# A linear-attention and SwiGLU block, two layers: the MLP's last product too by seven block products, in two passes of row tiles

## The chip, the cores and the metric

The kernel runs on one core of one Trainium2 chip. The metric is the device time of one execution in microseconds. Each kernel is run several times, and the median counts. One more execution of each kernel was profiled; durations and stalls quoted here come from that execution.

## The reference

```python
def _A_ref(x, wqkv, wo):            # S = 2048, D = 512, 32 heads of 16
    q, k, v = heads(x @ wqkv)
    phi = lambda t: where(t > 0, t + 1, exp(t)) + 1e-6
    pq, pk = phi(q), phi(k)
    kv = einsum("bhsd,bhse->bhde", pk, v)
    z = einsum("bhsd->bhd", pk)
    num = einsum("bhqd,bhde->bhqe", pq, kv)
    den = einsum("bhqd,bhd->bhq", pq, z)[..., None] + 1e-6
    return merge_heads(num / den) @ wo

def _B_ref(x, w1, w3, w2):          # F = 1792
    return (silu(x @ w1) * (x @ w3)) @ w2

x = A_x
x = x + _A_ref(_layernorm(x), A_wqkv, A_wo)
x = x + _B_ref(_layernorm(x), B_w1, B_w3, B_w2)
x = x + _A_ref(_layernorm(x), A_wqkv, A_wo)
x = x + _B_ref(_layernorm(x), B_w1, B_w3, B_w2)
```

All inputs are float32, and both layers use the same weights.

## The kernel before

Every float32 matrix is held as two float16 parts, a high and a low one, and each product runs as three float16 products (high by high, low by high, high by low; `PASSES`, `mm`). The high part is a copy on ScalarE, the low part a subtraction on VectorE (`split`).

The work goes in this order, twice: keys and the state (`attn_keys`, `state_in`, `state_out`), queries and weighing (`query`, `weigh`), attention output (`attn_out`), then the MLP. `pair` is one layer. In layer 0 a generator, `prepare`, converts weights in between, and during the MLP a second one, `background`, converts the rest; `PACE` says how many steps of them are put between two pieces of other work. The order that each engine gets comes from a scheduler in the framework, with priorities (`later` lowers one); TensorE then works in that order.

In the MLP, x has 16 tiles of 128 rows, in four chunks of four tiles (`NC`), and F has 14 tiles of 128, in seven groups of two (`NG`). One block of work is one group for one chunk; there are 28 in a layer. For w1 and w3 the kernel already uses the seven products of Winograd's form of Strassen's algorithm in place of eight: rows (`mlp_rows`) and weights (`w13_group`) are prepared as seven combinations each, and a block runs seven products P1 to P7 on three PSUM banks (`ba`, `bb`, `bc`), 12 matmuls of 256 columns each. ScalarE copies the bank `bb` out four times in a block (L740, L747, L750, L757), VectorE adds the other two (L744, L751, L755), and `swiglu` makes two halves of the hidden values, early and late: a tanh, two products, a copy and a subtraction (L709 to L714), 512 columns each.

The last product, by w2, is plain: `mlp_out` adds the block's hidden values times two tiles of w2 to four PSUM banks `po`, one for each row tile of the chunk, with 24 matmuls of 512 columns. TensorE does this one block later, between the seven products of the next one. After a set's last group `finish` adds each bank to x on VectorE (L832) and, in the end, stores the row tile (L836). Layer 0 runs the groups in two sets, 0 to 2 and 3 to 6, each for all chunks, so that weights can be converted during the first set; layer 1 runs all seven groups for one chunk after another. All 14 tiles of w2 stay in SBUF during an MLP.

DMAs go out through SyncE's queue in its own order: row transposes (L692, L697), raw weights (L334, L434), and rows kept in DRAM for a second set (L701, L779).

Of the kernel before, what the change touches and what calls it, by code (L numbers as in the profile page):

```python
# [45 lines left out]
GROUP = 14 * KB  # L46
AT_W = 0
AT_W2 = AT_W + NG * GROUP
AT_X = AT_W2 + 28 * KB
# [4 lines left out]
AT_H = AT_T + 4 * KB  # L54
AT_END = AT_H + 6 * KB
# [20 lines left out]
def kernel(  # L76
# [40 lines left out]
    def bank(name):  # L117
        return psum.tile([P, 512], F32, tag="w", name=name)

    nat_ring = Ring(view, *span(AT_NAT, 3), *span(AT_W2 + 16 * KB, 3))  # L120
# [5 lines left out]
            nat_ring,  # L126
# [4 lines left out]
            Ring(view, *span(AT_W2 + 16 * KB, 3)),  # L131
# [10 lines left out]
    t_ring = Ring(view, *span(AT_T, 2))  # L142
    h_ring = Ring(view, *span(AT_H, 3))
    xk_ring = Ring(view, *span(XB0 + 8 * KB, 3))
    xq_ring = Ring(view, *span(AT_W2 + 22 * KB, 3))
    pt_first = (*span(XB0 + 8 * KB, 3), XB1 + 12 * KB)
    pt_ring = Ring(view, *span(AT_W2 + 8 * KB, 4))
# [9 lines left out]
    ident = const.tile([P, P], F32, name="ident")  # L157
# [5 lines left out]
    mask = const.tile([P, P], F32, name="mask")  # L163
# [21 lines left out]
    wq_s = view(AT_W2, F16, 2, NK, D)  # L185
    wo_s = view(AT_W2 + 8 * KB, F16, 2, NK, D)
# [4 lines left out]
    w13 = [view(AT_W + g * GROUP, F16, 2, 2, 2, 7, P) for g in range(NG)]  # L191
    w2_s = [view(AT_W2 + f * 2 * KB, F16, 2, D) for f in range(NF)]
    st_att = [view(AT_W + at * KB, F32, NK, D) for at in (18, 0, 26, 34)]
    st_w13 = view(AT_W + 42 * KB, F32, 2, 2, 2, F)
    raw_at = {3: AT_W + 70 * KB, 4: AT_W + 78 * KB, 5: AT_W + 86 * KB, 6: rows_at[0]}
# [3 lines left out]
    w2_d = dram.tile([P, NF, 2, D], F16, name="w2_d")  # L199
# [127 lines left out]
    def load_raw(g):  # L327

        dst = view(raw_at[g], F32, 2, 2, 2, 2, P)
# [6 lines left out]
    def w13_group(g):  # L336

        dst = w13[g]
        if g in raw_at:
            raw = view(raw_at[g], F32, 2, 2, 4, P)  # L340
# [35 lines left out]
    def prepare():  # L376
# [37 lines left out]
        info["w2"] = weight_scale("w2", parts["w2"], 2.0**14)  # L414
        cb = scaled(info["w1"][1], 2.0**-9)
# [4 lines left out]
        for g in SETS[0]:  # L420
            yield from w13_group(g)
            state["groups"] = g + 1

    state = {"groups": 0, "tiles": 0, "rows": 0}
    w2_stage = (
        Ring(view, *span(AT_W2 + 24 * KB, 2)),
        Ring(view, *span(AT_W + 94 * KB, 2)),
    )

    def w2_pair(g):  # L430

        for f in (g, NG + g):
            r = w2_stage[g > SETS[0][-1]].next(F32, D)
            nc.sync.dma_start(r, w2_rows[:, f, :])  # L434
            split(w2_s[f][:, 0, :], w2_s[f][:, 1, :], r, info["w2"][2])
            yield 1
        state["tiles"] = g + 1

    def background():

        for g in SETS[0]:
            yield from w2_pair(g)
        for g in (3, 4, 5):
            load_raw(g)
        for g in SETS[1]:
            yield from w2_pair(g)
        nc.sync.dma_start(w2_d, view(AT_W2, F16, NF, 2, D))
        for g in SETS[1]:
            if g == 6:
                while state["rows"] < NC:  # L450
                    yield 100
                load_raw(6)
            yield from w13_group(g)
            state["groups"] = g + 1
# [9 lines left out]
    PACE = (3, 1, 2, 4)  # L464
# [17 lines left out]
    def attn_keys(layer, ready, prep, before_gram):  # L482
# [3 lines left out]
        pks = {}  # L486
        xts, nats = ready
# [19 lines left out]
        for t in range(NT):  # L507
# [4 lines left out]
            pk = h_ring.next(F16, 2, D)  # L512
# [7 lines left out]
            if t == 0:  # L520
                before_gram()
                gt += [acc_bank(f"gt{j}") for j in range(NK)]
                if layer == 0:
                    pz.append(bank("pz"))
# [467 lines left out]
```

## Time and profile before

| | |
|---|---|
| median of 3 runs | 1286.61 us (1285.42 to 1288.26) |
| profiled execution | 1289.51 us, of which the span of its instructions is 1287.8 us |
| TensorE (PE) busy | 1193.8 us, 93% |
| VectorE (DVE) busy | 722.6 us, 56% |
| ScalarE (ACT) busy | 605.8 us, 47% |
| GpSimd (POOL) busy | 269.0 us, 21% |
| mean granted TensorE clock | 0.97 |

Times of instructions count from the span's start. PE is the matmul part of TensorE, PEld its weight loads, SP the queue of SyncE. Matmuls are pipelined: one alone lasts longer than the distance to the next, so their cost is read from the distance. A line of a group gives the source line, engine, operation, what it writes and reads with the shapes, the count, the total and mean duration, and the idle time of the engine just before with what ended it. The line of a helper stands for all its callers: nearly all matmuls are L310.

### The profile page before, as it was taken

The numbers are of one execution on the slowest core, as the hardware profiler recorded it, in microseconds if no ns is written. First come the engines' busy times: TensorE is split into PE (matmuls) and PEld (weight loads), VectorE is DVE, ScalarE is ACT, GpSimd is POOL, SyncE is SP. The second block draws the span as 40 slices with busy tenths as digits, with TensorE's granted clock in tenths as the row PEclk, the third lists the DMA queues.
The fourth block names the chain that finished last, engine by engine and source line by source line (L and its number), as shares of the span: only waits on it lengthen the run. The fifth ranks groups of instructions, "written<-read, shape, count | busy, mean of one in ns | idle before, by whom it ended". The sixth has DMA issues, their size and how long they took to land.

```text
span 1287.8 us, 18971 instructions
## 1 busy us (share of the span) xinstructions
PE 1193.8 (93%) x7752; PEld 763.6 (59%) x7752; DVE 722.6 (56%) x1164; ACT 605.8 (47%) x1048; POOL 269.0 (21%) x264
## 2 busy tenths in 40 slices
PE   2999697678999999999999998989998999999998
PEld 1444343356767777777764443446776777777775
DVE  4968959884465345453544239784435345434444
ACT  5667667664343333433346645665334333333332
POOL 3310357163110000100004523675004001000000
PEclk9999899789999999999999998999998999999999
DMA  7976566375051101010216323565003003000000
GB/s 208 349 215 222 138 156 164 86 235 130 34 143 58 58 1 58 1 58 9 66 42 164 98 50 91 108 159 102 1 1 91 2 1 85 6 1 19 16 1 33
DMA packets 160520, 111.33 MB, mean 86 GB/s; under 512 B 129329, under 2 KB 137521, under 8 KB 158257
## 3 DMA queue, kind: packets, MB, share of 16 engines
q1 hardware_dynamic: 160432, 110.13, 31.9%
q8 instruction: 60, 0.98, 0.3%
q14 instruction: 28, 0.22, 0.1%
HBM read 50.86 MB, written 27.79 MB: 61 GB/s over the span
## 4 chain that ended last, share of the span: by engine, by line
PE 70%; DVE 8%; DMA 8%; POOL 7%; ACT 4%; issue 3%; SPq 0%; DVEq 0%; POOLq 0%; ACTq 0%
PE po L310 21%; PE bb L310 20%; PE bc L310 10%; PE pk L310 6%; PE gt L310 6%; DMA arena<-arena 5%; PE ba L310 5%; POOL arena L696 3%; DMA arena<-in_B_w_dram 1%; DVE arena L479 1%; DVE arena L583 1%; PE pq L310 1%; DVE arena L589 1%; DVE arena L244 1%; POOL arena L594 1%
## 5 line engine op out<-in xcount | busy, mean ns | idle before, releaser
L310 PEld LDWEIGHTS <-arena 128*128 128x128 f16 x7704 | 757.7, 99 | 502.4 <-issue 60.4
L310 PE MATMUL po<-arena 128*128 128x512 f16 x1728 | 428.7, 386 | 25.0 <-DMA arena<-arena 17.9
L310 PE MATMUL bb<-arena 128*128 128x256 f16 x2688 | 343.7, 276 | 11.5 <-ACT arena L750 6.3
L310 PE MATMUL bc<-arena 128*128 128x256 f16 x1344 | 165.5, 276 | 9.6 <-ACT arena L757 9.4
L751 DVE TENSOR_TENSOR arena<-arena,bc 128x512 f32<-128x512 f32 x56 | 38.4, 685 | 206.0 <-ACT arena L750 206.0
L714 DVE TENSOR_TENSOR arena<-arena 128x512 f16<-128x512 f32 x112 | 83.9, 749 | 87.7 <-ACT arena L713 87.3
L713 ACT ACTIVATE arena<-arena 128x512 f16<-128x512 f32 x112 | 70.2, 627 | 128.9 <-DVE arena L711 128.9
L750 ACT ACTIVATE arena<-bb 128x512 f32<-128x512 f32 x56 | 33.3, 594 | 200.3 <-PE bb L310 200.3
L710 DVE SCALAR_TENSOR_TENSOR arena<-arena 128x512 f32<-128x512 f32 x112 | 78.3, 699 | 79.8 <-ACT arena L709 79.5
L696 POOL TENSOR_TENSOR arena<-arena 128x512 f16<-128x512 f32 (+2 forms) x48 | 70.7, 1493 | 234.5 <-DMA arena<-arena 232.2
L244 DVE SCALAR_TENSOR_TENSOR arena<-arena,scalars 128x512 f16<-128x512 f32 (+2 forms) x110 | 89.5, 838 | 36.1 <-ACT arena L243 35.9
L709 ACT ACTIVATE arena<-arena,scalars 128x512 f32<-128x512 f32 x112 | 80.7, 721 | 58.4 <-DVE arena L751 42.0
L310 PE MATMUL pk<-arena 128*128 128x512 f16 x384 | 92.6, 394 | 15.2 <-ACT arena L243 8.8
L243 ACT ACTIVATE arena<-arena,scalars 128x512 f16<-128x512 f32 (+2 forms) x110 | 74.3, 717 | 42.9 <-DMA arena<-in_B_w_dram 18.3
L310 PE MATMUL gt<-arena 128*128 128x512 f16 x384 | 90.6, 384 | 2.1 <-ACT arena L243 2.1
L310 PE MATMUL pq<-arena 128*128 128x512 f16 x384 | 88.2, 379 | 0.0
L310 PE MATMUL ba<-arena 128*128 128x256 f16 x672 | 87.7, 273 | 0.0
L711 DVE SCALAR_TENSOR_TENSOR arena<-arena 128x512 f32<-128x512 f32 x112 | 79.4, 709 | 3.4
L757 ACT ACTIVATE arena<-bb 128x512 f32<-128x512 f32 x56 | 33.3, 595 | 66.0 <-PE bb L310 65.9
L287 ACT ACTIVATE arena<-arena,nb_all,rs_all 128x512 f32<-128x512 f32 x64 | 50.7, 805 | 25.3 <-POOL arena L696 13.8
L280 POOL TENSOR_SCALAR ve<-mv_all 128x4 f32<-128x4 f32 (+2 forms) x9 | 4.1, 451 | 278.8 <-DVE mv_all L273 267.4
L301 POOL TENSOR_TENSOR arena<-arena 128x512 f16<-128x512 f32 x31 | 37.9, 1227 | 93.1 <-ACT arena L300 91.7
(112 smaller groups left out, 903.9 us busy)
## 6 DMA issues: line engine op xcount, KB each, us to landing
xt_d<-arena SPq DMA_DIRECT2D x32, 256.0 KB, 3.0
arena<-xt_d SPq DMA_DIRECT2D x32, 256.0 KB, 2.8
arena<-in_B_w_dram SPq DMA_DIRECT2D x8, 896.0 KB, 7.1
arena<-in_B_w_dram SPq DMA_DIRECT2D x28, 256.0 KB, 3.2
xb_d<-arena SPq DMA_DIRECT2D x4, 1792.0 KB, 6.4
arena<-xb_d SPq DMA_DIRECT2D x4, 1792.0 KB, 6.8
arena<-in_A_x_dram SPq DMA_DIRECT2D x16, 256.0 KB, 5.7
arena<-in_B_w_dram SPq DMA_DIRECT2D x32, 128.0 KB, 3.1
```

Source lines behind the costliest of these rows:

```text
L243: nc.scalar.activation(hi, src, AF.Copy, scale=scale)
L244: nc.vector.scalar_tensor_tensor(lo, src, scale, hi, OP.mult, OP.subtract)
L287: nc.scalar.activation(dst, x_sb[:, t, :], AF.Identity, scale=rs_all[:, t : t + 1], bias=nb_all[:, t : t + 1],)
L301: engine.tensor_tensor(nat[:, 1, :], xn, nat[:, 0, :], OP.subtract)
L310: nc.tensor.matmul(dst, lhs(a, k), rhs(b, k), start=first and k == 0 and i == 0, stop=last and k == n - 1 and i == len(PASSES) - 1, skip_g ...
L696: nc.gpsimd.tensor_tensor(nat[:, 1, lo:hi, :], s, nat[:, 0, lo:hi, :], OP.subtract)
L709: nc.scalar.activation(t, gate, AF.Tanh, scale=info["half_u1"])
L710: nc.vector.scalar_tensor_tensor(t, t, 1.0, gate, OP.add, OP.mult)
L711: nc.vector.scalar_tensor_tensor(t, up, 2.0**-48, t, OP.mult, OP.mult)
L713: nc.scalar.activation(hs[:, 0], t, AF.Copy)
L714: nc.vector.tensor_tensor(hs[:, 1], t, hs[:, 0], OP.subtract)
L751: nc.vector.tensor_tensor(early[:, 1, :], early[:, 1, :], bc, OP.add)
```

## The change

The product by w2 is made by the same seven block products. The hidden values of a block (two row halves by two F tiles) give seven combinations, w2's two tiles by two column halves give seven, and each of the seven products, 256 columns wide, is summed over a set's groups in half a PSUM bank. For one row tile of each half that fills three and a half banks, and four are given to this work, so a chunk is run in two passes: one for the first row tile of each half, with every group as its hidden values become ready, two blocks late, and one for the second row tiles after the set's last group, for all groups of the set in a row. Only at the end of a pass are the seven sums combined and added to x (`mlp_add`). So hidden values are kept for a whole set, in slots of 7 KB.

For that space the weights can no longer all stay in SBUF: there are four slots for groups of w1 and w3 and five for groups of w2. Layer 0 runs sets of 3, 2 and 2 groups, layer 1 of 3 and 4; groups that are converted and needed again are stored in DRAM and fetched. Layer 1 now keeps its rows in DRAM too.

```diff
+OUT = (((0, 0), (3, 5)), ((4, 2), (5, 1)), ((1, 3), (2, 6)), ((6, 4),))
-SETS = ((0, 1, 2), (3, 4, 5, 6))
+SETS = (((0, 1, 2), (3, 4), (5, 6)), ((4, 5, 6), (3, 0, 1, 2)))
+SLOT13 = {0: 0, 1: 1, 2: 2, 3: 3, 4: 0, 5: 1, 6: 2}
+SLOT2 = {0: 3, 1: 4, 2: 2, 3: 0, 4: 1, 5: 3, 6: 4}
...
-    PACE = (3, 1, 2, 4)
+    PACE = (3, 1, 2, 3)
...
+    def w2_group(g):
+
+        raw = w2_stage.next(F32, 4, HALF)
+        for i, f in enumerate((g, NG + g)):
+            nc.sync.dma_start(raw[:, 2 * i : 2 * i + 2, :], w2_rows[:, f, :])
+        dst, scale = w2_s[g], info["w2"][2]
+        yield 1
+        split(dst[:, 0, 0], dst[:, 1, 0], raw[:, 0], scale)
+        yield 1
+        split(dst[:, 0, 1:3], dst[:, 1, 1:3], raw[:, 2:4], scale)
+        yield 1
+        a11, a21, a12, a22 = (raw[:, i] for i in range(4))
+        for to, a, b, op in (
+            (a22, a21, a22, OP.add),
+            (a21, a11, a21, OP.subtract),
+            (a11, a22, a11, OP.subtract),
+            (a12, a12, a11, OP.subtract),
+        ):
+            W2ENG.tensor_tensor(to, a, b, op)
+        yield 1
+        split(dst[:, 0, 3:], dst[:, 1, 3:], raw, scale)
...
+    def background(first):
+
+        yield from first
+        a, b, c = SETS[0]
+        for g in a:
+            yield from w2_group(g)
+            store("w2", g, view(AT_W2 + SLOT2[g] * GROUP2, F16, GROUP2 // 2))
+        late = view(AT_W + 3 * GROUP, F16, 2, 2, 2, 7, P)
+        for g in b[::-1]:
+            load_raw(g)
+            if g == b[-1]:
+                for i in a:
+                    store("w13", i, view(AT_W + i * GROUP, F16, GROUP // 2))
             yield 1
+            yield from w13_group(g, late)
+            if g == b[-1]:
+                store("w13", g, view(AT_W + 3 * GROUP, F16, GROUP // 2))
+            have.add(("w13", g))
+            yield from w2_group(g)
+        while state["set"] < 1:
+            yield 100
+        for g in c:
+            load_raw(g)
+            yield 1
+            yield from w13_group(g, w13[g])
...
+    W2ENG = nc.gpsimd
+    TENG = (nc.vector, nc.vector)
...
+    def hidden_parts(hs, t, lo, hi):
+        nc.scalar.activation(hs[:, 0, lo:hi], t[:, lo:hi], AF.Copy)
+        nc.vector.tensor_tensor(hs[:, 1, lo:hi], t[:, lo:hi], hs[:, 0, lo:hi], OP.subtract)
+
+    def hidden(engine, hs, t, late):
+        swiglu(late, t[:, 2:4])
+        hidden_parts(hs, t, 0, 2)
+        b11, b22, b12, b21, t1, t2, t4 = (t[:, i] for i in range(7))
+        engine.tensor_tensor(t1, b12, b11, OP.subtract)
+        engine.tensor_tensor(t2, b22, t1, OP.subtract)
+        engine.tensor_tensor(b12, b22, b12, OP.subtract)
+        engine.tensor_tensor(t4, b21, t2, OP.subtract)
+        hidden_parts(hs, t, 2, 7)
...
-    def mlp_out(g, h, is_late, po, tiles, ends):
-        for i in tiles:
-            half, sub = divmod(i, 2)
...
+    def mlp_out(sub, g, hs, acc, ends):
+
+        cs = slice(sub * P, (sub + 1) * P)
+        w2 = w2_s[g]
+        for a, bs in ((0, (0, 1)), (1, (0,))):
+            for po, pair in zip(acc, OUT):
+                for i, (qw, qx) in enumerate(pair):
+                    for b in bs:
+                        nc.tensor.matmul(
+                            po[:, i * HALF : (i + 1) * HALF],
+                            hs[:, a, qx, cs],
+                            w2[:, b, qw, :],
...
+    def mlp_add(sub, c, acc, engine):
...
+        def add(dst, src, to):
+            nc.vector.scalar_tensor_tensor(dst, src, cb, to, OP.mult, OP.add)
+
+        nc.scalar.activation(u[:, 0], a0[:, :HALF], AF.Copy, scale=cb)
+        add(x0, a2.rearrange("p (h n) -> p h n", h=2), x0)
+        add(x1, a3[:, None, :HALF].to_broadcast([P, 2, HALF]), x1)
+        add(x1[:, 0], a1[:, HALF:], x1[:, 0])
+        add(u[:, 1], a0[:, HALF:], u[:, 0])
+        add(u[:, 2], a1[:, :HALF], u[:, 1])
+        engine.tensor_tensor(x0, x0, u[:, 0::2], OP.add)
+        engine.tensor_tensor(x1, x1, u[:, 1:], OP.add)
...
+                def middle(at_, i=i, first=at == 0 and i == 0):
+                    if first:
+                        first_pending(at_)
+                    if at_ == 0 and len(waiting) > 1:
+                        first_half(waiting.pop(0))
+                    if at_ == 2 and done:
+                        ends.append(second_half())
+                    if at_ == 3 and ends:
+                        ends.pop()()
...
+    def moves(layer, gs, i):
+
+        if layer == 0 and gs is SETS[0][0] and i == 0:
+            fetch("w13", 4, 0)
+        if layer == 1 and gs is SETS[1][0]:
+            fetch("w13", i, i)
+            if i == 0:
+                fetch("w2", 0, 2)
```

In the built program of the changed kernel, lines have new numbers: L322 is `mm`, L833 the products by w2, L764 to L770 `swiglu` and its splits, L776 to L779 the four differences, L851 and L853 the adds at the end of a half, L859 and L860 the two sums on the engine that is passed in (GpSimd, and VectorE for the last half).

More of the change, by code (lines that the diff above doesn't have):

```diff
@@ L811, in pair, with first_pending @@
                     steps(prep, PACE[1] if t < 9 else PACE[2])
-        more = background() if layer == 0 else iter(())
+        more = background(prep) if layer == 0 else iter(())
         def ready_for(what, g):
-            for source in (prep, more):
-                while state[what] <= g and next(source, None) is not None:
-                    pass
-        def pending(i):
+            while layer == 0 and (what, g) not in have:
+                next(more)
+        def first_pending(i):
             if i < 2:
```

296 lines of the change are left out of this document (161 added, 135 removed).

## The prediction

> **What bounds the kernel now.** I read the engine summary, then the two MLP stretches as time windows, then the order of instructions inside one block, then the groups by shape.
>
> ```profile
> PE 1193.8 (93%) x7752; PEld 763.6 (59%) x7752; DVE 722.6 (56%) x1164; ACT 605.8 (47%) x1048; POOL 269.0 (21%) x264
> ...
> 200.00:264.00 64.00, 47.73 (x236) 25.30 (x237) 57.37 (x102) 45.27 (x87) 23.34 (x21) 0.84 0.48 123
> 264.00:290.00 26.00, 17.99 (x110) 11.83 (x109) 22.73 (x24) 17.80 (x28) 20.56 (x17) 0.87 0.80 252
> 290.00:500.00 210.00, 203.62 (x1502) 148.27 (x1500) 103.75 (x154) 79.55 (x131) 19.35 (x18) 0.98 0.23 65
> 500.00:678.00 178.00, 175.69 (x1301) 127.09 (x1299) 87.04 (x145) 65.80 (x108) 14.32 (x17) 1.00 0.14 42
> ...
> 884.00:1277.00 393.00, 387.96 (x2888) 283.26 (x2886) 176.00 (x256) 144.74 (x237) 35.70 (x31) 0.99 0.09 21
> ```
>
> Columns of the windows: length, busy time of PE, PEld, DVE, ACT, POOL, clock, DMA. The first block of MLP one ends at 264, the second at 290; its last at 678; MLP two runs from 884 to 1277. In 884:1277 PE misses 5 us of 393: product time is the bound there. In 200:264 it is not: DVE is busy 57 of 64 us, PE 48, at a clock of 0.84.
>
> ```profile
> 1007.66 0.68 DVE L744 TENSOR_TENSOR arena<-arena,ba 128x512 f32<-128x512 f32 x1
> ...
> 1008.59 1.47 PE L310 MATMUL bb<-arena 128*128 128x256 f16 x12
> ...
> 1009.90 1.89 PE L310 MATMUL po<-arena 128*128 128x512 f16 x8
> ...
> 1011.63 0.60 PE L310 MATMUL bb<-arena 128*128 128x256 f16 x4
> ```
>
> Twelve products of 256 columns take 1009.90 − 1008.59 = 1.31 us, 109 ns each; eight of 512 take 1.73, 216 each. So a block now is 84 × 0.109 + 24 × 0.216 = 9.17 + 5.19 = 14.36 us.
>
> ```profile
> L714 DVE TENSOR_TENSOR arena<-arena 128x512 f16<-128x512 f32 x112 | 83.9, 749 | 87.7 <-ACT arena L713 87.3
> ...
> L751 DVE TENSOR_TENSOR arena<-arena,bc 128x512 f32<-128x512 f32 x56 | 38.4, 685 | 206.0 <-ACT arena L750 206.0
> ```
>
> **PE, the gain.** 42 products of 256 columns replace 24 of 512: 42 × 0.109 = 4.58 us, so a block is 13.75, 0.61 less; 56 blocks, 34 us. That is the ceiling if nothing else becomes late.
>
> **DVE, the price.** L714, both inputs in SBUF, takes 692 ns where POOL rests (its mean from 1100 to 1180 us); so 0.16 fixed and 0.53 for 512 columns. A block gains four differences of 256 columns (0.43 each) and 768 more columns to split (0.80): 2.5 us on the 6.0 that it costs now. L832 (744 ns, 48 times) goes; each half of a run of groups ends instead in five PSUM adds, two at 0.74 and three at an estimated 0.48, 2.9 us: 24 halves in layer 0, 16 in layer 1. A w2 group splits 1792 columns in place of 1024 (2.5 us against 1.5). Layer 1 so needs 28 × 8.5 + 47 = 285 us of DVE in some 380: still PE's. Layer 0 needs about 123 us more than its 213 of 264:678, 85%, and unevenly. Counted in the order of the built program, the 14 blocks of 290:500 hold 279 DVE instructions worth 193 us by these durations. Independent ones start some 80 ns before the last ends (0.59 us from one to the next at 1007), which returns 11 if half of them are.
>
> POOL takes the four differences of each w2 group and two x-updates per half; that stretch gets some 75 us of POOL work instead of 19. L714's mean is 749 ns against 692 alone, while L751, one input in PSUM, stays at 685: SBUF pairs stretch beside POOL. I take 1.5 us a block. Bounds: 0, and all 75 us (5.4 a block). The SBUF page (the Trainium skill, SBUF — State Buffer, Who interferes with whom) says that the ports are locked exclusively and the loser waits in full; by that the upper bound would hold, and the trace agrees as to which rows stretch.
>
> The ordering leaves DVE waiting for the 1280-column copy and for tanh in most blocks: I take 1.5 us (L709 is 0.72; L691 is 0.62 at 512 columns and 1.05 at 1024, so 1.25 at 1280). ACT itself is not the bound: 80 us of 210 now, and some 140 then.
>
> **New waits and moved steps.** The adds share one buffer of three 256-column parts: L853 on ACT waits until POOL has summed the half before, and behind it on ACT stand the copies that free PE's banks. A half is 4.6 us of products or more after the one before, and POOL's two sums take some 2.6 (L519, 1.33 each), so I take nothing; where POOL stands behind L753, which waits for a transpose landing (3.9 us), that cover is gone, three times in layer 0, inside the +47 below. On SP the raw weights of groups 3 to 6 and of w2 share one 8 KB buffer, so their loads wait for splits and stand ahead of the row transposes; a chunk's rows take some 33 us of copies, differences and transposes, and a pass of three groups lasts 41. Four more stores and reloads of rows (6.4 and 6.8 us) and 14 weight moves (seven stores and seven fetches, 10 MB each way) go beside products: nothing, by a DMA of 0.09 to 0.23 there; without that cover 7 us each. In layer 1 the gram starts two tiles later, with the first tiles' key products in front.
>
> **Stage by stage, against the span of 1287.8.**
> - Up to 264: the built order puts 19 fewer splits and eight fewer differences, 20 us of DVE, ahead of the first block's end. PE there waits partly for transposes; I take −6 (−12 to 0).
> - 264:290: the second block has 12 us of DVE work instead of 22.7: 14 us instead of 26, −12 (−14 to −4).
> - 290:500: 193 − 11 + 21 + 21 = 224 against 210, +13. If DVE's waits and POOL hide, PE sets 14 × 13.75 + 6.4 of present idle = 199, −11; with POOL in full 193 − 11 + 75 = 257, +47.
> - 500:678: 12 blocks need 12 to 13 us of DVE each: PE's, 165 us plus 4 of waits, −8 (−10 to +3). Two-group sets are tight: blocks without a second half have 9.17 + 2.29 = 11.46 us of PE.
> - 678:884: two first halves and one second half are outstanding (9.2 us of products, now 5.2); PE idles 13 us there: +1 (−3 to +5).
> - 884:1277: 27 × 9.17 + 28 × 4.58 − 8.3 left for the tail = 367.6. Waits: 5 now, 6 more for eight hand-overs of the four accumulation banks and for row preparation in passes of 41 us instead of 100. 379, −14 (−20 to −3).
> - The tail: now four adds, then the store.
>
> ```profile
> 1281.83 2.73 DVE L832 SCALAR_TENSOR_TENSOR arena<-po,scalars,arena 128x512 f32<-128x512 f32 x4 [0.84 <-PE po L310]
> 1282.61 2.31 SPq L836 DMA_DIRECT2D out_dram<-arena  x4
> ```
>
>   After: the last hidden values need add 0.7, tanh 0.7, two products 1.4, four differences 1.8, copy 1.25, split 1.5; then 12 to 38 products, then ten adds and four sums on DVE, some 7.7 us in place of 2.73. From the last P3, 21 us instead of 11: +10 (+6 to +13).
>
> Sum: −6 −12 +13 −8 +1 −14 +10 = −16: span 1271.8. The profiled execution is 1289.5, 0.2% above the median of 1286.61; against the median, 1270.6.
>
> **Rivals.**
> 1. *DVE and POOL take turns in layer 0's first set*, so 290:500 costs +47 and the whole +18, 1305. It decides from +29 in that stage. For it: L714's stretch and 75 us of POOL. Against: a third of DVE's work there reads PSUM.
> 2. *The accumulation banks come free late.* The second half takes the four banks that the first half's adds are still reading; between stand P3 and P5, 2.6 us, and the adds take 2.9 behind a tanh chain. I allow 0.5 us for each hand-over; with 2.8 for each of the 20 runs it is 46 more, 1317. For it: DVE's load. Against: the built order moves products ahead of the second half.
> 3. *Narrow products cost more than half a wide one.* The gain is gone at 5.19 / 42 = 124 ns. At 133 ns every block takes 42 × 24 ns = 1.0 us more than forecast, 56 us in all: −16 + 56 = +40, 1327. Against: 109 ns where PE runs them back to back, weight loads of 99 ns (757.7 us over 7704) included. TensorE: Matmul & The Clock Gate (the Trainium skill, Back-to-back issue gap) speaks against the change: it gives a sustained 131 ns at 512 columns and 81 at 128. An estimate of 98 at 256 from these would make a block 42 × 98 − 24 × 131 ns = +1.0 us, +54 in place of −34. The trace disagrees, with 216 and 109.
> 4. *DVE keeps up everywhere*: 290:500 at 199, the whole −40, 1247.
> 5. *The terms cancel*: within 2.6 us of now.
>
> **How the numbers follow.** Forecast (−30 to −3) 0.43, rival 4 0.14, rival 5 0.05, rival 1 0.24, rival 2 0.10, rival 3 0.04. Faster 0.57, same 0.05, slower 0.38; 0.2%, 2.6 us, is what a measurement can tell. The range reaches from rival 4 to just past rival 1: 1244 to 1309; the forecast's own is 1257 to 1284.
>
> **What would show it.** Right: product groups with 2352 products of 256 columns spaced at 109 ns; MLP two some 14 us shorter with PE over 97% busy; DVE over 85% busy in the first dozen blocks and PE waiting on it there; the second block early; a tail near 21 us. Wrong: PE waits on DVE in MLP two, waits at the start of second halves of 2 us and more, L851 behind POOL, or ACT queued behind L853.

## The result, and the profile after

The changed kernel takes 1292.03 us (median of 7 runs, 1290.96 to 1295.69), the kernel before 1286.94 (7 runs, 1285.42 to 1288.26): ratio 1.0044, 95% interval 1.0033 to 1.0056. It is 5.1 us slower, where 16 faster had been forecast. The profiled execution took 1290.96, its span 1289.2.

The page of the changed kernel: the engine summary, VectorE's busy share in 40 slices, and the shares of the chain that ended last.

```profile
PE 1164.3 (90%) x8760; PEld 858.2 (67%) x8760; DVE 989.6 (77%) x1551; ACT 662.9 (51%) x1095; POOL 412.9 (32%) x368
...
DVE  4968959689887898888986339685788777778676
...
PE 47%; DVE 29%; ACT 7%; DMA 6%; POOL 5%; issue 4%; SPq 1%; DVEq 0%; POOLq 0%; ACTq 0%
```

VectorE's row and the chain of the kernel before:

```profile
DVE  4968959884465345453544239784435345434444
...
PE 70%; DVE 8%; DMA 8%; POOL 7%; ACT 4%; issue 3%; SPq 0%; DVEq 0%; POOLq 0%; ACTq 0%
```

PE has 29.5 us less to do and VectorE 267 us more (722.6 before). VectorE's row has a plateau of 7 to 9 in layer 0's MLP (the ninth to the 21st slice), where it had mostly 3 to 6. The chain that ended last ran 70% over PE and 8% over VectorE before, now 47% and 29%.

Time windows by stage (length, busy time of PE, PEld, DVE, ACT, POOL, clock, DMA share, GB/s). The stages are cut where VectorE starts to add P3's bank in a block (L818; L755 before): from 200 up to the first block's, to the second block's, blocks 1 to 15, blocks 15 to 27, MLP two.

```profile
200.00:252.40 52.40, 44.29 (x236) 24.16 (x237) 40.36 (x75) 32.96 (x70) 29.19 (x28) 0.90 0.51 144
252.40:273.40 21.00, 14.40 (x103) 11.14 (x102) 16.73 (x20) 13.93 (x23) 15.72 (x15) 0.76 0.99 285
273.40:506.60 233.20, 204.15 (x1780) 174.07 (x1778) 205.73 (x285) 114.05 (x172) 78.30 (x61) 0.99 0.34 102
506.60:678.80 172.20, 166.66 (x1492) 145.05 (x1491) 149.19 (x241) 75.57 (x117) 42.36 (x36) 1.00 0.21 71
889.60:1268.40 378.80, 367.46 (x3334) 326.43 (x3334) 286.38 (x424) 167.05 (x250) 80.66 (x58) 1.00 0.23 74
```

In MLP two PE is busy 367.5 of 378.8 us: the products are the bound, as they were. Between blocks 1 and 15 VectorE is busy 205.7 of 233.2 (104.5 of 210.8 before), PE 204.2: that the bound has changed hands there is what the experiments test.

| Stage | before | after | measured | forecast |
|---|---|---|---|---|
| up to block 0's P3 | 263.6 | 252.4 | −11.2 | −6 |
| block 0 to 1 | 26.0 | 21.0 | −5.1 | −12 |
| blocks 1 to 15 | 210.8 | 233.2 | +22.4 | +13 |
| blocks 15 to 27 | 177.6 | 172.2 | −5.4 | −8 |
| 27 to 28, attention 2 | 205.9 | 210.8 | +4.9 | +1 |
| 28 to 55, MLP two | 392.8 | 378.8 | −14.0 | −14 |
| tail | 11.1 | 20.9 | +9.7 | +10 |
| span | 1287.8 | 1289.2 | +1.4 | −16 |

The order of PE's products in MLP two, start and length of each group:

```profile
1108.13 1.47 PE L322 MATMUL bb<-arena 128*128 128x256 f16 x12
1109.44 1.58 PE L833 MATMUL po<-arena 128*128 128x256 f16 x13
1110.86 1.36 PE L322 MATMUL bb<-arena 128*128 128x256 f16 x11
```

Twelve products of the first kind start 1.31 us before the next group, thirteen of the second 1.42: 109 ns each, in both. The narrow products cost what was forecast. Then the groups that answer to those shown of before (all of the kernel; the last figure of a line is the engine's idle time before the group, and what ended it):

```profile
L833 PE MATMUL po<-arena 128*128 128x256 f16 x2352 | 293.6, 275 | 38.9 <-ACT arena L769 32.7 <-DVE arena L851 4.3 <-DVE arena L770 1.5
...
L770 DVE TENSOR_TENSOR arena<-arena 128x512 f16<-128x512 f32 x112 | 132.8, 1186 | 81.2 <-ACT arena L769 80.6
...
L766 DVE SCALAR_TENSOR_TENSOR arena<-arena 128x512 f32<-128x512 f32 x112 | 98.9, 883 | 2.7
...
L814 DVE TENSOR_TENSOR arena<-arena,bc 128x512 f32<-128x512 f32 x56 | 38.1, 681 | 10.8 <-ACT arena L813 10.8
```

L770 (L714 before) handles 1792 columns a block instead of 1024. L766, two inputs in SBUF, has a mean of 883 ns; L814 (L751 before), one input in PSUM, stays at 681 (685). PE's idle time before the products by w2 is 38.9 us, of which 32.7 end with ScalarE's copy of hidden values and only 4.3 with an add that frees an accumulation bank.

The built order gives the blocks of this stage between 95 and 175 products each in place of 126, so a long block need not be a late one. Block 3 is the longest (23.7 us; its 175 products are 19.1 us at 109 ns). Its timeline shows how the price is paid:

```profile
310.11 2.60 POOL L753 TENSOR_TENSOR arena<-arena 128x1024 f16<-128x1024 f32 x1 [0.54 <-ACT arena L748]
...
311.04 2.22 DVE L766 SCALAR_TENSOR_TENSOR arena<-arena 128x512 f32<-128x512 f32 x1
...
312.67 1.71 POOL L859 TENSOR_TENSOR arena<-arena 128x512 f32<-128x512 f32 x1
313.30 1.37 DVE L776 TENSOR_TENSOR arena<-arena 128x256 f32<-128x256 f32 x1
...
314.70 1.37 DVE L777 TENSOR_TENSOR arena<-arena 128x256 f32<-128x256 f32 x1
...
318.00 0.94 DVE L779 TENSOR_TENSOR arena<-arena 128x256 f32<-128x256 f32 x1
...
318.86 0.68 DVE L807 TENSOR_TENSOR arena<-arena,ba 128x512 f32<-128x512 f32 x1
318.97 1.27 ACT L769 ACTIVATE arena<-arena 128x1280 f16<-128x1280 f32 x1 [5.73 <-DVE arena L779]
...
319.59 1.47 PE L322 MATMUL ba<-arena 128*128 128x256 f16 x12 [2.67 <-DVE arena L807]
```

While GpSimd prepares rows and sums x, L766 takes 2.22 us (0.69 where GpSimd rests) and the differences L776 and L777 take 1.37 each (0.42). L807, which frees PE's bank, reads PSUM and takes its usual 0.68, but it stands behind them in VectorE's order: PE's next product waits 2.67 us for it, and ScalarE's copy of the hidden values 5.73 for the differences.

The tail:

```profile
1271.75 0.42 DVE L776 TENSOR_TENSOR arena<-arena 128x256 f32<-128x256 f32 x1
...
1273.34 1.27 ACT L769 ACTIVATE arena<-arena 128x1280 f16<-128x1280 f32 x1 [3.07 <-DVE arena L779]
...
1274.66 4.32 PE L833 MATMUL po<-arena 128*128 128x256 f16 x38 [2.07 <-ACT arena L769]
...
1278.26 4.29 DVE L851 SCALAR_TENSOR_TENSOR arena<-po,scalars,arena 128x512 f32<-128x512 f32 x8 [2.13 <-PE po L833]
...
1285.50 0.68 DVE L860 TENSOR_TENSOR arena<-arena 128x512 f32<-128x512 f32 x1
```

Four differences, a copy and a split stand between the last hidden values and their products; after these VectorE adds from 1278.26 to 1286.2. This is as forecast, step by step.

### The profile page after: what moved, and what is told of

The parts are those of the page before. It is cut to its first block, busy times and chain, and to the rows that moved or that the text cites. A ratio compares the mean times of both kernels' runs of the same rounds, so it can differ in the third digit from the quotient of the medians.

```text
span 1289.2 us, 21685 instructions
## 1 busy us (share of the span) xinstructions
PE 1164.3 (90%) x8760; PEld 858.2 (67%) x8760; DVE 989.6 (77%) x1551; ACT 662.9 (51%) x1095; POOL 412.9 (32%) x368
## 4 chain that ended last, share of the span: by engine, by line
PE 47%; DVE 29%; ACT 7%; DMA 6%; POOL 5%; issue 4%; SPq 1%; DVEq 0%; POOLq 0%; ACTq 0%
PE po L833 11%; PE bb L322 11%; PE pk L322 6%; PE gt L322 6%; PE bc L322 6%; DMA arena<-arena 5%; DVE arena L851 4%; DVE arena L770 3%; DVE arena L766 3%; DVE arena L765 3%; ACT arena L769 3%; PE po L322 3%; PE ba L322 2%; DVE arena L256 2%; POOL arena L753 2%
## 5 line engine op out<-in xcount | busy, mean ns | idle before, releaser
L322 PEld LDWEIGHTS <-arena 128*128 128x128 f16 x6360 | 623.1, 99 | 322.9 <-issue 57.9
L322 PE MATMUL bb<-arena 128*128 128x256 f16 x2688 | 334.4, 275 | 15.2 <-ACT arena L810 11.5
L833 PE MATMUL po<-arena 128*128 128x256 f16 x2352 | 293.6, 275 | 38.9 <-ACT arena L769 32.7
L833 PEld LDWEIGHTS <-arena 128*128 128x128 f16 x2352 | 229.4, 99 | 78.2 <-ACT arena L769 41.3
L859 POOL TENSOR_TENSOR arena<-arena 128x512 f32<-128x512 f32 x38 | 56.8, 1495 | 451.6 <-DVE arena L851 309.6
L770 DVE TENSOR_TENSOR arena<-arena 128x512 f16<-128x512 f32 x112 | 132.8, 1186 | 81.2 <-ACT arena L769 80.6
L769 ACT ACTIVATE arena<-arena 128x512 f16<-128x512 f32 x112 | 106.2, 948 | 137.3 <-DVE arena L779 70.6
L322 PE MATMUL bc<-arena 128*128 128x256 f16 x1344 | 161.1, 273 | 3.0 <-DVE arena L814 1.9
L256 DVE SCALAR_TENSOR_TENSOR arena<-arena,scalars 128x512 f16<-128x512 f32 (+2 forms) x117 | 103.2, 901 | 33.0 <-ACT arena L255 30.9
L765 DVE SCALAR_TENSOR_TENSOR arena<-arena 128x512 f32<-128x512 f32 x112 | 91.7, 818 | 43.2 <-ACT arena L764 43.1
L764 ACT ACTIVATE arena<-arena,scalars 128x512 f32<-128x512 f32 x112 | 80.6, 720 | 85.7 <-DVE arena L814 60.4
L851 DVE SCALAR_TENSOR_TENSOR arena<-po,scalars,arena 128x256 f32<-128x256 f32 (+1 forms) x200 | 107.9, 582 | 4.4 <-PE po L833 3.4
L322 PE MATMUL po<-arena 128*128 128x512 f16 x384 | 95.3, 405 | 11.4 <-DMA arena<-arena 11.4
L322 PE MATMUL pk<-arena 128*128 128x512 f16 x384 | 91.8, 391 | 10.9 <-ACT arena L255 8.3
L753 POOL TENSOR_TENSOR arena<-arena 128x512 f16<-128x512 f32 (+2 forms) x48 | 72.7, 1532 | 89.3 <-DMA arena<-arena 80.6
L766 DVE SCALAR_TENSOR_TENSOR arena<-arena 128x512 f32<-128x512 f32 x112 | 98.9, 883 | 2.7
L810 ACT ACTIVATE arena<-bb 128x512 f32<-128x512 f32 x56 | 33.3, 594 | 124.1 <-DVE arena L766 85.4
L322 PE MATMUL gt<-arena 128*128 128x512 f16 x384 | 88.9, 379 | 2.2 <-ACT arena L255 2.1
L322 PE MATMUL pq<-arena 128*128 128x512 f16 x384 | 88.4, 379 | 0.9 <-ACT arena L532 0.9
L322 PE MATMUL ba<-arena 128*128 128x256 f16 x672 | 84.3, 273 | 3.6 <-DVE arena L807 3.5
L860 POOL TENSOR_TENSOR arena<-arena 128x512 f32<-128x512 f32 x38 | 61.8, 1627 | 0.0
```

The lines of the kernel that those rows point to most:

```text
L256: nc.vector.scalar_tensor_tensor(lo, src, scale, hi, OP.mult, OP.subtract)
L322: nc.tensor.matmul(dst, lhs(a, k), rhs(b, k), start=first and k == 0 and i == 0, stop=last and k == n - 1 and i == len(PASSES) - 1, skip_g ...
L753: nc.gpsimd.tensor_tensor(nat[:, 1, lo:hi, :], s, nat[:, 0, lo:hi, :], OP.subtract)
L764: nc.scalar.activation(t, gate, AF.Tanh, scale=info["half_u1"])
L765: nc.vector.scalar_tensor_tensor(t, t, 1.0, gate, OP.add, OP.mult)
L766: nc.vector.scalar_tensor_tensor(t, up, 2.0**-50, t, OP.mult, OP.mult)
```

## The experiments

The theory: PE's gain is real in every block, and VectorE takes it back in layer 0's first set, by the volume of its work (A) and by what GpSimd's work beside it adds to each instruction with two SBUF inputs (B). The rivals: accumulation banks that come free late (C), the chain of raw-weight loads through one 8 KB buffer (D), rows that are late (E). Each build orders its instructions anew, so single stages move by some us for that alone, and each row of the table is one profiled execution. "Stage" is blocks 1 to 15; "out" means that the kernel leaves that work out.

| Kernel | span | stage | PE | VectorE | GpSimd (busy in it) |
|---|---|---|---|---|---|
| before | 1287.8 | 210.8 | 204.4 | 104.5 | 19.8 |
| changed | 1289.2 | 233.2 | 204.2 | 205.7 | 78.3 |
| sums on VectorE | 1286.9 | 225.6 | 199.0 | 201.0 | 46.0 |
| sums out | 1275.7 | 222.9 | 201.2 | 190.3 | 45.0 |
| differences out | 1268.4 | 217.1 | 199.0 | 177.5 | 78.3 |
| differences on GpSimd | 1301.0 | 240.2 | 204.9 | 187.2 | 126.5 |
| groups 3, 4 not made | 1274.6 | 223.3 | 204.7 | 186.0 | 80.4 |
| rows out | 1265.5 | 216.7 | 198.9 | 193.3 | 53.8 |
| sums, differences, groups out | 1252.9 | 208.4 | 197.7 | 147.8 | 44.9 |
| all four out | 1241.0 | 201.5 | 197.3 | 142.1 | 11.3 |

**The closing sums on VectorE** (e1_sums_dve)

```diff
-            mlp_add(sub, c, acc, nc.vector if last_one else nc.gpsimd)
+            mlp_add(sub, c, acc, nc.vector)
```

> The two closing x-sums of every half (L859, L860) go from GpSimd to VectorE; nothing else is edited. In the changed kernel the stretch between the second and the sixteenth block of layer 0 (blocks 1 to 15) lasts 233.2 us, with 20 such sums, 33.5 us on GpSimd, in it. Theory A, the volume of VectorE's work sets that stretch: 20 sums of 0.69 us are 14 us more on it, some 8 us of stretching beside GpSimd go: 239 us. Theory B, sharing between VectorE and GpSimd sets it (the loser waits in full): 33 us of sharing go, 14 come: 214 us. Theory C, hand-over of the accumulation banks: the sums come after the banks are free: 231 to 235 us. The 40 to 55 stretch (205.7 us, product-bound) stays in all three within 1 us.

225.6 us, between A (239) and B (214). VectorE takes on 20 sums of 0.735 us, 14.7 us, and yet is busy 4.7 us less. VectorE's groups in the stage, first the changed kernel, then this one:

```profile
L765 DVE SCALAR_TENSOR_TENSOR arena<-arena 128x512 f32<-128x512 f32 x28 | 22.1, 790 | 6.0 <-ACT arena L764 6.0
...
L777 DVE TENSOR_TENSOR arena<-arena 128x256 f32<-128x256 f32 x14 | 9.6, 685 | 0.4
```

```profile
L765 DVE SCALAR_TENSOR_TENSOR arena<-arena 128x512 f32<-128x512 f32 x28 | 19.8, 707 | 3.8 <-ACT arena L764 3.8
...
L859 DVE TENSOR_TENSOR arena<-arena 128x512 f32<-128x512 f32 x10 | 7.3, 735 | 0.0
...
L777 DVE TENSOR_TENSOR arena<-arena 128x256 f32<-128x256 f32 x14 | 6.7, 479 | 0.3
```

The same instructions take 790 and 707 ns, 685 and 479. Summed over the stage's instructions, what each takes beyond the median of its shape where GpSimd rests fell from 30.0 to 16.4 us, for 32 us less of GpSimd's work: 0.42 us for each (0.56 had been used in expectations below, from busy times alone). Neither volume nor sharing alone accounts for the result; both are there.

**The closing sums left out** (e4_no_sums)

```diff
-        engine.tensor_tensor(x0, x0, u[:, 0::2], OP.add)
-        engine.tensor_tensor(x1, x1, u[:, 1:], OP.add)
+        if engine is nc.vector:
+            engine.tensor_tensor(x0, x0, u[:, 0::2], OP.add)
+            engine.tensor_tensor(x1, x1, u[:, 1:], OP.add)
```

> Leaves out the two closing x-sums of every half but the last chunk of the kernel, so that x lacks these parts: GpSimd loses some 120 us of the whole, 33.5 between blocks 1 and 15, and no other engine gets them. Theory A (VectorE's volume): only the stretching of VectorE's instructions beside them goes, some 8 us: 225 us for blocks 1 to 15. Theory B (sharing in full): 33 us go: 200 us. Theory C (banks): 233. The difference to the run with the sums on VectorE is the price of the sums themselves there, 14 us by theory A.

222.9, close to A's 225. With e1, the sums themselves cost the stage only 2.7 us on VectorE (14 by A); what they cost on GpSimd, 10.3 us, is for the most part sharing.

**The hidden differences left out in layer 0** (e2_no_diffs)

```diff
+    nc.gpsimd.memset(view(AT_T + 4 * KB, F32, 3, HALF), 0.0)
...
-    TENG = (nc.vector, nc.vector)
+    TENG = (None, nc.vector)
...
+        if engine is not None:
...
```

> Leaves out the four differences of the hidden values (L776 to L779) in layer 0; three of the seven hidden parts are zeros set once at the start there. In the stretch of blocks 1 to 15 they take 34.7 us of VectorE (56 instructions, 620 ns). Theory A (VectorE's volume): 233.2 falls by most of it, to 202 to 208 us, where the products' 199 take over. Theory B (sharing): GpSimd keeps its 78 us of work and VectorE has less beside it: about 215. Theory C (banks): unchanged but for a shorter chain to the second product: 228 to 234. Theory D (a serial chain through the 8 KB buffer of raw weights and its loads): 230 or more.

217.1: 16 of the 34.7 us came back, less than A had (202 to 208), about what B had. D is out with its 230, and C with its 228: no load and no bank was touched. VectorE's busy time falls by 28.2, so 12 of that was not on the path: once it is relieved, more blocks are bound by the products (PE is busy over 97% of blocks 6 to 9 and 14, in the changed kernel only of 8 and 9). The edit also shortens the chain to the hidden values by four steps, so this run alone does not part VectorE's volume from the length of that chain.

**Groups 3 and 4 not made** (e3_no_conv)

```diff
-            load_raw(g)
...
+            nc.sync.dma_start(
+                view(AT_W + 3 * GROUP, F16, GROUP // 2), view(AT_W + 1 * GROUP, F16, GROUP // 2)
+            )
...
-            yield from w13_group(g, late)
+            yield 13
...
-            yield from w2_group(g)
+            nc.sync.dma_start(
+                view(AT_W2 + SLOT2[g] * GROUP2, F16, GROUP2 // 2),
+                view(AT_W2 + SLOT2[2] * GROUP2, F16, GROUP2 // 2),
+            )
+            yield 6
+            have.add(("w2", g))
```

> Leaves out the making of groups 3 and 4 while the first set runs: their weights are copied by DMA from groups 1 and 2, so that no raw load, no split and no difference is made for them. That is about 20 us less on VectorE (two first-product groups of 7.5, two second-product groups of 2.5), 16 on ScalarE, 8 on GpSimd between blocks 1 and 15. Theory A (VectorE's volume): 233.2 falls to 211 to 215 us. Theory B (sharing): 8 us of GpSimd go, and 20 of VectorE with them: 208 to 215, not told apart here. Theory C (banks): 230 to 235. Theory D (the serial chain of raw loads): PE's 199 to 205. In the chain of blocks 15 to 27 (172.2 us) nothing changes but groups 5 and 6: within 3 us.

223.3: 10 us back, half of what A expected, and far from D's 199 to 205. The chain of raw loads does not set this stage. VectorE's busy time fell by the expected 20 us, and here the chain to the hidden values kept all its steps: work that lies beside that chain is worth these 10 us (6 us of ScalarE's copies went with it).

**The hidden differences on GpSimd** (e5_diffs_pool)

```diff
-    TENG = (nc.vector, nc.vector)
+    TENG = (nc.gpsimd, nc.vector)
```

> The four differences of the hidden values go from VectorE to GpSimd in layer 0, nothing else. Between blocks 1 and 15 that takes 34.7 us from VectorE and gives GpSimd some 60 (56 of 1.1 us, by L742 to L745). Theory A+B (volume and sharing together, with 0.56 us of stretch on VectorE for each us of GpSimd work, from the run with the sums on VectorE): 34 us of stretch replace the 34.7: the stretch of blocks 1 to 15 stays at 228 to 240 us (233.2 in the changed kernel), the whole within 10 us of it. Volume alone, without sharing: 200 to 206. Chains alone (GpSimd's 1.1 us in place of 0.62, four in a row, in each block): 235 to 245.

240.2 us, the whole 11.8 slower. VectorE has less to do (187.2 us busy: 34.7 went, some 12 of stretch came on the other instructions) and the stage is longer all the same: VectorE stands idle for 53 us of it. 240.2 is at the upper end of A+B's 228 to 240 and inside the 235 to 245 of its rival, the chain of four GpSimd differences in a row; the idle time speaks for the chain, which no run took apart. The place of work counts beside its volume.

**Three left out together** (e6_all_three_out: the edits of e2, e3 and e4)

> Leaves out together what was left out one by one: the closing x-sums (but the last chunk's), the four hidden differences of layer 0, and the making of groups 3 and 4. One by one they gave 10, 16 and 10 us of the 34 that blocks 1 to 15 last beyond the products' 199. Theory A+B (VectorE's volume, stretched by sharing): VectorE falls to some 130 us in the stretch, and it lasts 199 to 205: the products are the bound again. Theory C or D (hand-overs, serial loads, which stay): 212 or more, with VectorE idle a third of the time.

```profile
266.50:474.90 208.40, 197.70 (x1785) 173.86 (x1784) 147.82 (x211) 107.19 (x163) 44.91 (x39) 1.00 0.39 120
```

208.4: below C's and D's 212, above A+B's 205. PE now has 10.7 us of idle time left.

**Rows left out** (e8_no_rows)

```diff
-                    rows = mlp_rows(layer, c + 1)
+                    rows = reload_rows(c + 1) if layer == 0 else mlp_rows(layer, c + 1)
...
-        nc.sync.dma_start(view((XB0, XB1)[c % 2], F16, 2, 14, HALF), xb_d[:, c])
+        nc.sync.dma_start(view((XB0, XB1)[c % 2], F16, 2, 14, HALF), xb_d[:, 0])
```

> Leaves out the preparation of the rows of chunks 1 to 3 in layer 0 (normalising, differences, halves, transposes): every chunk there loads the first chunk's rows again. That takes 29 us of GpSimd between blocks 1 and 15, ScalarE's copies for it and six transposes, and none of VectorE's own work. Theory A+B: 29 x 0.56 = 16 us of stretch go: 217 us in place of 233.2. Theory E, the rows themselves are late and hold the blocks up: the three blocks that start a chunk (19.2, 23.7 and 18.5 us) fall to 14, 218 or less, with waits for loaded rows gone from PE. Theory A without sharing: 230 to 234. Block 0 (21.0 us), which holds half of chunk 1's preparation, falls to 14 to 17 by A+B.

216.7, A+B's 217, although not one VectorE instruction was taken out: VectorE's busy time fell by 12.4 us, all of it stretch. The other 4.1 us are less idle time of VectorE; ScalarE's row copies, gone too, may account for them. Of the three blocks that E would bring to 14, one took 10.8, the others 17.6 and 18.2, but these two hold 159 and 167 products, 17.3 and 18.2 us at 109 ns, so that this does not decide on E. The changed kernel's own trace does: of the 27.7 us that PE waits in this stage, 14.8 end with ScalarE's copy of hidden values, 2.0 with an add that frees an accumulation bank, and none with a DMA. Block 0 took 18.1 us where 14 to 17 had been expected, with 121 products in it in place of 101.

**All four left out** (e9_all_four_out: the edits of e2, e3, e4 and e8)

> Leaves out sums, hidden differences, the making of groups 3 and 4, as the run with three left out did (208.4 us for blocks 1 to 15, VectorE 148 us busy), and the row preparation of chunks 1 to 3 of layer 0 too. If what was left over the products' 199 there was GpSimd's and ScalarE's row work, 199 to 203 (199 at a granted clock of 0.99 or 1.00); if it is the hand-over of banks and hidden values, 206 to 209. Block 0, 21.0 us in the changed kernel, 22.4 with three left out and 18.1 without rows, falls to 14 to 16 if VectorE and the rows between them set it.

```profile
265.50:467.00 201.50, 197.31 (x1779) 174.35 (x1778) 142.06 (x207) 95.35 (x145) 11.27 (x12) 0.99 0.26 93
```

201.5 us with PE busy 197.3: the stage is the products' again. Blocks 3 to 11 take 13.2 to 15.1. The second half's hand-over of banks, untouched here, adds next to nothing, and neither does the wait for hidden values, though their chain is four steps shorter here. Block 0 did not follow: it stays at 20.9, but with 18.4 us of PE's work in it in place of 14.4, so it says little.

**Work moved off GpSimd** (f1_less_pool) and **placed by the runs** (f2_placed); nothing is left out.

```diff
-            mlp_add(sub, c, acc, nc.vector if last_one else nc.gpsimd)
+            mlp_add(sub, c, acc, nc.vector)
...
-    W2ENG = nc.gpsimd
+    W2ENG = nc.vector
...
-            nc.gpsimd.tensor_tensor(t[:, 0, :], b12, b11, OP.subtract)
+            nc.vector.tensor_tensor(t[:, 0, :], b12, b11, OP.subtract)
...
```

> What GpSimd does in the MLPs goes to VectorE as far as it is cheaper there: the closing x-sums (0.735 us instead of 1.68), the differences of the second weights (0.45 instead of 0.95) and the four differences of the row preparation (0.43 instead of 1.1). Theory A+B: between blocks 1 and 15 VectorE gets 14 + 8.5 + 5 us and loses 65 x 0.56 = 36 of stretch: 9 us less than 233.2, and the first blocks of layer 1 lose 2 to 4 more; the whole 1278 to 1286 us. Sharing alone as the bound: 200 to 210 for that stretch, 1262. Volume alone: 250 to 260, 1310.

1283.54 us, ratio to before 0.9967 (0.9953 to 0.998): the sign is turned, with the stage at 224.7 as expected. VectorE is as busy as in the changed kernel (204.9 us) with GpSimd at 17.6: the stretch was replaced by work. The second run puts single pieces back on GpSimd:

```diff
+            one = nc.gpsimd if layer == 0 and final and c == NC - 1 else nc.vector
+            mlp_add(sub, c, acc, nc.gpsimd if last_one and sub == 0 else one, last_one and sub == 0)
...
+        u = view(rows_at[0] if other else AT_UV, F32, 3, HALF)
...
+            rd = nc.vector if layer == 0 else nc.gpsimd
```

> Each piece of GpSimd's MLP work goes where the runs so far had it cheaper, nothing is left out: the closing x-sums on VectorE (in the run with them there the stretch of blocks 1 to 15 lasted 225.7 us and the first twelve blocks of layer 1 171.1, against 233.2 and 173.1), but on GpSimd for the last chunk of layer 0, which ends inside attention 2 (214 us there with VectorE, 210.8 with GpSimd); the differences of the second weights and, in layer 0 alone, of the rows on VectorE (4 us less up to the first block, 4 us more in layer 1 in the run with them there). In the last chunk the first half's sums stay on GpSimd with a buffer of their own, so that VectorE has 1.4 us less at the end. Sum against the changed kernel's 1292: -4 -1 -8.5 -0 +0 -2 -1.5 = -17: 1275 us, by theory A+B. If the gains of the single runs came from the order of the built program and not from where the work is, they need not add up: 1280 to 1290.

1279.67 us, ratio 0.994 (0.992 to 0.9961): faster, but the gains did not add up to 1275. Attention 2 stayed at 213.9 and the tail at 21.5, neither better than with the work on VectorE; the row work of layer 1 did give back its 3.8 us.

**The gate by one ScalarE function** (f3_silu on f2_placed, g2_after_silu on the changed kernel, g1_before_silu on the kernel before)

```diff
-        nc.scalar.activation(t, gate, AF.Tanh, scale=info["half_u1"])
-        nc.vector.scalar_tensor_tensor(t, t, 1.0, gate, OP.add, OP.mult)
-        nc.vector.scalar_tensor_tensor(t, up, 2.0**-50, t, OP.mult, OP.mult)
+        nc.scalar.activation(t, gate, AF.Silu, scale=info["half_u1"])
+        nc.vector.scalar_tensor_tensor(t, up, 2.0**-21, t, OP.mult, OP.mult)
...
-        info["half_u1"] = scaled(info["w1"][1], 2.0**-22)
+        info["half_u1"] = scaled(info["w1"][1], 2.0**-21)
...
-        cb = scaled(info["w1"][1], 2.0**-5)
-        nc.vector.tensor_tensor(cb, cb, info["w3"][1], OP.mult)
+        cb = scaled(info["w3"][1], 2.0**-12)
```

In the kernel before the powers are 2^-48 and 2^-19, 2^-9 and 2^-16. With this function the hidden values carry w1's own scale, which had cancelled before, so the powers rest on the size of these weights.

> As the run before it in this call, and the gate is taken by one ScalarE function (Silu) in place of Tanh and a VectorE step (L765): 1.4 us less VectorE work in each block (two of 0.69), and none more for another engine but for some loads of ScalarE's table where attention and MLP overlap. Between blocks 1 and 15 that is 20 us of VectorE. Theory A (its volume is the bound there): 224 becomes 208 to 214 us; blocks 15 to 27 and layer 1, where the products are the bound, gain under 3 us together; the tail loses 0.7 of its chain. The whole 1258 to 1266. Theory C or D: within 4 us of the run before it.

1258.96 us (1257.81 to 1264.46), ratio 0.9793 (0.9771 to 0.9814): the fastest of the kernels that leave nothing out. Its engine summary and chain:

```profile
PE 1155.2 (92%) x8760; PEld 860.4 (68%) x8760; DVE 912.3 (73%) x1568; ACT 671.4 (53%) x1100; POOL 249.3 (20%) x238
...
PE 67%; DVE 16%; ACT 6%; DMA 5%; issue 3%; POOL 2%; SPq 1%; DVEq 0%; POOLq 0%; ACTq 0%
```

The stage fell by 11 us from 227.5, to 216.5 (208 to 214 expected), and blocks 15 to 27 by 6, where under 3 had been expected for these and layer 1 together: VectorE's work holds PE up there too. Then the same edit on the two kernels that the prediction compares:

> The kernel before, with the gate by one ScalarE function (Silu) in place of Tanh and a VectorE step (two of 0.69 us less in each block). Theory A: its MLP stretches are product-bound (VectorE 105 of 211 us busy between blocks 1 and 15), so they gain nothing there: 209 to 212 us; the tail loses 0.7 of its chain and some stalls go: 1282 to 1287 us in all. Rival: shorter chains help either kernel alike, because hidden values that come late hold PE up: then 10 to 20 us here too, 1265 to 1277.

> The changed kernel, all of GpSimd's work left where it is, with the same one edit. Theory A+B: 28 VectorE instructions of 0.79 us go between blocks 1 and 15, 22 us: 233.2 becomes 211 to 218 us; blocks 15 to 27 gain 4 to 6 as in the run with both edits; the whole 1264 to 1272. Beside the kernel before with the same edit that is 12 to 20 us faster: the change then brings what had been forecast for it (16 us), and its sign hangs on VectorE's volume in layer 0's first set. Rival: as the kernel before, or 4 to 5 us slower again, since the two keep their distance whatever VectorE does.

| | before | changed | changed − before |
|---|---|---|---|
| as they were (median) | 1286.94 | 1292.03 | +5.1 |
| gate by one function (median) | 1280.32 | 1264.45 | −15.9 |

Ratios to the kernel before, measured beside them: 0.9946 (0.9932 to 0.996) and 0.9822 (0.9808 to 0.9836). Windows of blocks 1 to 15, first the kernel before with the edit, then the changed one with it:

```profile
286.10:497.20 211.10, 204.81 (x1500) 149.06 (x1500) 86.37 (x127) 81.61 (x132) 21.24 (x20) 0.98 0.25 73
```

```profile
269.30:487.90 218.60, 200.29 (x1771) 173.58 (x1769) 181.49 (x256) 115.67 (x173) 79.42 (x63) 0.98 0.40 116
```

Taking the same two instructions out of each block leaves the kernel before at 211.1 us in this stage (210.8), and takes the changed one from 233.2 to 218.6 (211 to 218 expected). What it gained elsewhere in the kernel before, 6.6 us, is more than the 0 to 5 expected (1.6 up to the first block, 1.9 in block 0, 3.5 in MLP two). The distance between the two kernels does not stay: it turns from +5.1 to −15.9. In the spans it moves by 19.2 us: 14.9 in this stage and 6.1 in blocks 15 to 27 (172.2 to 166.1; 177.6 in the kernel before, with and without the edit), while the other stages give 1.8 back. The edit also takes one step out of the chain to the hidden values; that volume counts apart from this chain rests on the run without groups 3 and 4.

## Why the prediction was wrong, by its own steps

- **PE, the gain: right.** 109 ns a product; blocks 40 to 55 run at 13.71 us each (205.7 / 15) against the 13.75 worked out, and MLP two takes 378.8 against 379. Rival 3, narrow products that cost more, is out.
- **The tail: right**, +9.7 of +10, by the steps named.
- **290:500, the term that turned the sign: mis-sized.** Its sum was 193 − 11 + 21 + 21 = 224. Taken apart in the same way, the 233.2 us are 176 of VectorE's work at its undisturbed durations (182 forecast), 30.0 of stretch beside GpSimd (21 forecast) and 27.5 of VectorE's idle time (21 forecast). The stretch is summed as in the first experiment. I had taken 21 of 75; it was 30 of 78. The idle time is waits for ScalarE's copies and tanh, as argued, only more of them. That the stage would be VectorE's, and which rows would stretch, was right. e1, e4 and e8 show the stretch, e3 the volume (e2 and e6 with a shorter chain beside it), e9 that little is left over the products when these and the row work are out. For blocks 0 to 27 the prediction had 213 + 123 = 336 us of VectorE's work, which is 81% of their 414 us before and not the 85% that it states; VectorE was busy 371.7 of 426.4 us.
- **264:290: mis-sized.** VectorE's work was to set it, 12 us, so 14. It took 21.0. VectorE was busy 16.7 us, some 5 of them stretch, summed as above; the forecast of this stage had no term for that. PE waits 3.50 us for a ScalarE copy that frees its bank, and 2.90 for the hidden values. The timeline shows a chain behind the first wait, akin to the one that I had described (L853 on ScalarE, waiting for GpSimd) and priced at nothing:

```profile
256.10 5.09 POOL L753 TENSOR_TENSOR arena<-arena 128x512 f16<-128x512 f32 x3 [1.06 <-DMA arena<-arena]
...
257.62 0.81 ACT L299 ACTIVATE arena<-arena,nb_all,rs_all 128x512 f32<-128x512 f32 x1 [1.76 <-POOL arena L753]
...
260.64 0.58 ACT L810 ACTIVATE arena<-bb 128x512 f32<-128x512 f32 x1
261.27 2.72 PE L322 MATMUL bb<-arena 128*128 128x256 f16 x12 [3.50 <-ACT arena L810]
```

  GpSimd's L753 takes 5.09 us; ScalarE's row normalising (L299) needs the buffer that it reads and waits; behind it on ScalarE stands L810, which frees PE's bank, and PE waits 3.50. ScalarE's order is only the last part of that wait: L810 writes a buffer that VectorE's L766 reads until 259.21, late behind an L765 that took 1.64 us in place of 0.69. This is read off the trace; no run took it out alone. The granted clock was 0.76 in that window (0.87 before), and the twelve products at 261.27 take 2.72 us where 1.47 is usual.
- **678:884: mis-sized.** 4 us of products carried over from MLP one were to fill 13 us of PE's idle time. PE's busy time rose by 3.1 us and its idle time did not shrink (13.2 before, 15.1 after): +4.9, the upper end.
- **500:678** gave 5.4 of the 8 (the gate by one function took 6 us more out of it, so VectorE holds part of it too), and **up to 264** 11.2 where 6 was taken, inside its bounds.
- **The sum.** Against −16 the spans say +1.4: 9.4 from 290:500, 6.9 from 264:290, 3.9 from attention 2, 2.6 from 500:678, less 5.2 at the start. Another 3.7 us lie between spans and medians: the profiled execution of before was 2.6 above its seven-run median, that of the changed kernel some 1.1 below its own.
- **Rival 1**, VectorE and GpSimd in turns, had the mechanism and too high a price on VectorE: of 62 us beside GpSimd its instructions lost 30.0, not all, and GpSimd's lost 18.5. Taking turns makes both wait, so the whole 75 us on VectorE did not follow from it. **Rival 2** is out: 4.3 us of waits for banks in the whole kernel, where it had 46 beyond the forecast's 0.5 for each of 20 hand-overs. **Rival 4**'s 199 was come near only with VectorE's work down to 142 us (e9). **Rival 5**, within 2.6 us, came closest in number and was missed by 2.5.

What stays open: how much of the stage differences of 2 to 5 us among the runs is the order that each build chose, and what sets attention 2, which took 205 to 217 us over the runs, with none made for it.

## What to carry to other kernels

A gain on the busiest engine counts stage by stage: ask for each stage what the next engine needs, at its stretched durations and with its waits; here 88% busy was already the bound. Before paying for PE's time with VectorE instructions, look for VectorE instructions that another engine can do: here one function on ScalarE was worth 28 us to the changed kernel and 7 to the one before. A serial buffer or an in-order queue behind a GpSimd instruction needs a price even where its usual cover is long.

## What the runs showed of the hardware

GpSimd slows VectorE by kind of operand. In the changed kernel L766 (512 columns, both inputs in SBUF) takes 691 ns where GpSimd rests and 1583 where it works throughout (medians of 75 and 14), L777 425 and 1102; L814 and L851 (256 columns), with an input in PSUM, 680 and 678, 475 and 473; L644, a reduction of one SBUF input, 671 and 674. The Trainium skill (SBUF — State Buffer, Who interferes with whom) says that a VectorE instruction with two SBUF inputs contends with a GpSimd instruction that reads SBUF, that one with at most one SBUF input, outside the two-port modes, does not, and that the two contend for an exclusive lock. The trace agrees on who is slowed. How the loss divides, the runs show: between blocks 1 and 15 the two-input instructions ran 62 us beside GpSimd's and lost 30.0, about half. GpSimd waits too: its 60 instructions in that stage took 18.5 us beyond the medians of their shapes where no such VectorE instruction runs (1.27 us for a sum of 512 columns, of which the stage has 20, with means of 1.58 in L859 and 1.77 in L860). The two losses together are 48.5 of the 62 us. So VectorE's half speed does not speak against engines that take turns, and whether they do so in full stays open; GpSimd's spans in the profile are rough.

The Silu function took 719 ns for 512 columns, Tanh 717. With it ScalarE loaded a function table six times in the kernel before and four times in the changed one, 1.28 us each; with Tanh it did so once.
